# Moving the row-maximum subtraction to GpSimd and the exponential behind the transpose, with scratch rows stored in residue order

## The chip, the cores and the metric

The kernel runs on one core of one Trainium2 chip. A core has a matrix engine (TensorE, in the profile PE, with its weight loads as PEld), VectorE (DVE), ScalarE (ACT), GpSimd (POOL) and SyncE (SP), which here only issues DMAs. The metric is the device time of one execution in microseconds. The kernel before takes 710.51 us as the median of 3 runs (709.28 to 711.08).

## The reference

Two layers follow each other. The first is attention over 8 batches of 8 heads, 576 positions and 64 features per head. Four heads see a window of 32 positions back; the other four see every fourth position, 32 of them back. The second is a mixture of 8 experts: each of the 4608 tokens goes to one expert, in the order of its gate values, with at most 576 tokens for an expert.

```
mask_plain = (rel >= 0) & (rel < window)
mask_dil = (rel >= 0) & (rel < window * dilation) & (rel % dilation == 0)
scores = np.where(masks[None, :, :, :], scores, -1000000000.0)
scores = scores - np.max(scores, axis=-1, keepdims=True)
attn = np.exp(scores)
attn = attn / (np.sum(attn, axis=-1, keepdims=True) + 1e-09)
...
x = attn_out.transpose(0, 2, 1, 3).reshape(B * S, H * D)
...
h = np.maximum(x[mask] @ w1[e], 0.0)
out[mask] = h @ w2[e]
```

## The kernel before, in words

**Attention.** The work is cut into 32 units: 8 batches, two kinds of heads (kind 0 the plain window, kind 1 the dilated one), and two pairs of heads for each kind. Two heads lie on the two halves of the 128 partitions. A unit's 576 query rows are 9 chunks of 64 rows, and each chunk sees 96 keys. For kind 1 the host has sorted the positions by their remainder modulo 4 (the residue), so that a dilated window becomes a plain one; its rows therefore come out in residue order, while those of kind 0 are in token order.

The steps of a unit, with the names of their buffers and their lines: PE multiplies queries and keys into `pm` (`scores`, L380, chunks 0 to 4 and then 5 to 8); DVE adds the mask, scales, negates and takes the row's extreme in one instruction for each chunk (`most`, L386), which leaves the scores in `sc` and the extremes in `mx`; ACT takes the exponential of each chunk in place, with the extreme as its bias (`exps`, L392, nine instructions of 128x96); PE transposes `sc` three chunks at a time into `pS` (`turn`, L396); ACT copies that to `et` (L250, three of 96x384); PE multiplies `et` with the values, in whose tile a column of ones gives the row sums (`values`, L402, into `px`); DVE divides (`weigh`, L408 and L409) into `xs`. The pools have 3 tiles of `sc` and 3 of `et`.

When both units of a kind are done, SP stores `xs` to the scratch tensor `xd` in DRAM (`stores`), from which the second layer gathers rows later. PE also transposes `xs` (L463), ACT copies that to `xt` (on DVE, L477, at the very end), and PE multiplies `xt` with the gate weights (L497, L516, L552). The rows of kind 0 go to `xd` with two DMAs (L432). The rows of kind 1 have to be put back from residue order to token order, which takes 20 DMAs for a batch (L441): ten pieces, in which the chunk, the residue and the place in it stay the same, for each of the two halves of the partitions. The copy to `xt` puts them back in the same way, in two instructions each time.

**Routing and experts.** After the last gate value, DVE and PE search for the first expert's threshold (`alone`), lay out the list of its tokens (`digits`, `by_chunk` L952 on POOL, `by_row` L956 on ACT, `within` L960 on DVE, `place` L967 on PE, `indices` L976 to L979), and POOL gathers the token rows from `xd` with five indirect DMAs (L1131). The expert's weights come in 256 KB pieces into the tiles `raw` (SP, L1032), which lie in memory that attention used. ACT and DVE split them into a high and a low part (`w1h`, `w1l`, `w2h`, `w2l`, L1014 and L1015; some low parts by DMAs from POOL, L1042), PE multiplies (L1182, L1224), and POOL scatters the rows to the output with the same indices (L1250). Eight rounds of this follow each other.

**What sets the order.** Every step is an `Op` with an engine, a cost that is written in the code, and what it depends on. The planner (`Schedule.run`) plays the steps through with these costs and due times, and writes each engine's instructions down in the order that comes out. On the chip an engine takes its instructions in just that order and waits at each until its inputs are there. SP's queue is such an order too: a store that waits holds back the loads behind it. The loads of a batch go to one of two sets of `q`, `k` and `v` tiles, and wait until the batch before the last is done with it.

Of the kernel before, what the change touches and what calls it, by code (L numbers as in the profile page):

```python
# [25 lines left out]
NB = S // 64  # L26
SR = S // DIL
NCH = N // 128
NEG = -1e30
LG = 12  # L30
NK = 16
# [11 lines left out]
B_C = (0, 2500, 20000, 20000, 20000, 20000, 20000, 20000)  # L43
P_U, B_A, B_T, B_K, B_V, B_P, TOL_A, TOL_B, TOL_C, TOL_D = 4500, 8000, 4000, -5200, 4000, -105500, 650, 650, 300, 800
GR, N_S, N_E = ((0, 5), (5, 9)), 3, 3
MSZ = (128, 128, 128, 128, 64)
# [8 lines left out]


def consts():

# [3 lines left out]
    for kind in range(2):  # L62
        m = np.zeros((2, QB, NB, KB), np.float32)
        for c, (q0, k0) in enumerate(starts()):
            q, k = q0 + np.arange(QB)[:, None], k0 + np.arange(KB)[None, :]
# [160 lines left out]
def attention(tc, ctx, C, load_const, T, xd, Lt, R):  # L226
# [84 lines left out]
    class Unit:  # L311
# [16 lines left out]
        def build(self):  # L328
# [60 lines left out]

        def exps(self, c0, c1, mx, sc):  # L390
            for c in range(c0, c1):
                nc.scalar.activation(sc[:, c], sc[:, c], AF.Exp, bias=mx[:, c:c + 1], scale=-1.0)  # L392

# [17 lines left out]

    def pieces():

        out, at = [], 0
        while at < S:
            c, q = divmod(at, QB)
            r, i = divmod(at, SR)
            n = min(QB - q, SR - i)
            while q == 0 and n % QB == 0 and n + QB <= SR - i:
                n += QB  # L420
            out.append((c, q, r, i, n))
            at += n
        return out

    def stores(b, kind, xs):
        xb = xd[b * S:(b + 1) * S]
        out = []
        for half in range(2):
            f0 = 256 * kind + 128 * half
            src = xs[half * 64:half * 64 + 64].rearrange("p c a d -> p c (a d)")  # L430
            if kind == 0:
                out.append((lambda f0=f0, src=src: nc.sync.dma_start(  # L432
                    xb[:, f0:f0 + 128].rearrange("(c i) x -> i c x", i=QB), src), 64 * NB * 512))
                continue
            for c, q, r, i, n in pieces():
                k = -(-n // QB)
                w = min(n, QB)

                def put(c=c, q=q, r=r, i=i, k=k, w=w, src=src, f0=f0):
                    rows = xb[:, f0:f0 + 128].rearrange("(i r) x -> r i x", r=DIL)[r, i:i + k * w]  # L440
                    nc.sync.dma_start(rows.rearrange("(c i) x -> i c x", c=k), src[q:q + w, c:c + k])  # L441

                out.append((put, n * 512))
        return out
# [3 lines left out]
    def banks(un, xs, done, usex):  # L448
# [8 lines left out]
        for i in range(3):  # L457
            pt = Buf(PV)

            def turn(i=i, pt=pt):  # L460
                t = pt.tile[:, :384].rearrange("p (a c i) -> p a c i", a=2, c=3)
                for c in range(3):
                    nc.tensor.transpose(t[:, :, c], xs[:, 3 * i + c].rearrange("p a d -> p (a d)"), C["identf"])  # L463

            eng = "DVE" if b == B - 1 and kind and i else "ACT"

            def keep(i=i, pt=pt, f=nc.vector.tensor_copy if eng == "DVE" else act):
                t = pt.tile[:, :384].rearrange("p (a n) -> p a n", a=2)
                if kind == 0:
                    f(xt[:, :, 192 * i:192 * i + 192], t)  # L470
                    return
                x = xt.rearrange("p a (i r) -> p a r i", r=DIL)
                at = 0
                while at < 192:
                    r, j = divmod(192 * i + at, SR)
                    n = min(192 - at, SR - j)
                    f(x[:, :, r, j:j + n], t[:, :, at:at + n])  # L477
                    at += n
# [4 lines left out]
            k = un.op(eng, (450 if kind == 0 else 520) + 100 * (eng == "DVE"), keep, [t, *oldt], late)  # L483
            pt.users.append(k)
            xt_[b].append(k)
# [128 lines left out]
class Router:  # L614
# [355 lines left out]
    def indices(self, ps):  # L970
# [10 lines left out]
        return idx  # L981


def moe(tc, ctx, C, R, xd, w1, w2, out):
# [119 lines left out]
    def listing(r, sl):  # L1104
# [60 lines left out]
    def expert(r, X, box, W1, W2):  # L1165
# [48 lines left out]
        for m, n in sorted(enumerate(MSZ), key=lambda x: x[1] if r == NE - 1 else 0):  # L1214
# [33 lines left out]
            def put(m=m, n=n, y=y):  # L1248
                nc.gpsimd.memset(spacer, 0.0)
                s = nc.gpsimd.indirect_dma_start(  # L1250
                    out=out, out_offset=bass.IndirectOffsetOnAxis(ap=box[0][:n, m:m + 1], axis=0),
                    in_=y[:n], in_offset=None)
# [3 lines left out]

            usey.append(op("POOL", 1200, put, [c], B_S, lat=2300))

# [3 lines left out]

    X, BOX, W, EN = {}, {}, {}, {}

    def round_(r):
# [3 lines left out]
        en = st["fetch"] = EN[r] = op("SP", 100, lambda: fetch(r, R.eidx), [e])  # L1269
        ix, BOX[r] = settle(r, e)  # L1270
        X[r] = gather(r, ix, BOX[r])
        W[r] = [weights("1", r, f, [en]) for f in range(NF)]
# [15 lines left out]
def layout(inputs):  # L1288
# [7 lines left out]
    d = {  # L1296
        "in_qp": plain(q), "in_kp": plain(k),
        "in_qd": plain(apart(q)), "in_kd": plain(apart(k)),
# [58 lines left out]
```

## Time and profile before

| What | Value |
|---|---|
| median of 3 runs | 710.51 us |
| profiled execution, its time and its span | 706.26 us, 704.5 us |
| busy: PE, DVE, ACT, POOL | 652.6, 458.7, 341.1, 113.2 us |
| mean granted TensorE clock | 0.966 |
| exponentials L392 | 288 instructions, 81.5 us busy, 367 ns each |
| copies to `et` L250 | 96 instructions, 43.3 us busy, 485 ns each |
| mask and extreme L386 | 288 instructions, 253 ns each |
| stores of attention rows, L432 and L441 | 16 and 160 DMAs |

The span falls into three stages: attention up to about 197 us, where the last gate values are multiplied; routing for the first expert up to 230 us, where the first gather is issued; and the experts to the end. The profiled execution ran 4.25 us (0.6%) below the median of the others. PE's busy time is counted to the modelled end of each pipelined matmul, so that 98% busy still holds small gaps.

### The profile page before, as it was taken

The numbers are of one execution on the slowest core, as the hardware profiler recorded it, in microseconds if no ns is written. First come the engines' busy times: TensorE is split into PE (matmuls) and PEld (weight loads), VectorE is DVE, ScalarE is ACT, GpSimd is POOL, SyncE is SP. The second block draws the span as 40 slices with busy tenths as digits, with TensorE's granted clock in tenths as the row PEclk, the third lists the DMA queues.
The fourth block names the chain that finished last, engine by engine and source line by source line (L and its number), as shares of the span: only waits on it lengthen the run. The fifth ranks groups of instructions, "written<-read, shape, count | busy, mean of one in ns | idle before, by whom it ended". The sixth has DMA issues, their size and how long they took to land.

```text
span 704.5 us, 17467 instructions
## 1 busy us (share of the span) xinstructions
PE 652.6 (93%) x6553; PEld 556.9 (79%) x6553; DVE 458.7 (65%) x1939; ACT 341.1 (48%) x891; POOL 113.2 (16%) x162
## 2 busy tenths in 40 slices
PE   8789999998952899999999999999999999999995
PEld 5678788877741698798789789879978978988983
DVE  3537566665566699688589779868978955723300
ACT  5767897867601474376235333523524525424210
POOL 0000000000000332542311310310311131211011
PEclk9979999999965899999999999999999999999998
DMA  8996886795532684897213513511621484112001
GB/s 238 268 259 173 257 220 198 202 268 158 138 88 78 202 180 105 250 221 234 98 54 122 186 60 113 188 45 51 226 85 54 150 277 150 51 55 97 1 24 45
DMA packets 69882, 103.35 MB, mean 147 GB/s; under 512 B 8355, under 2 KB 41123, under 8 KB 69795
## 3 DMA queue, kind: packets, MB, share of 16 engines
q1 hardware_dynamic: 60454, 77.07, 37.1%
q0 software_dynamic: 9344, 25.17, 12.9%
q8 instruction: 51, 0.84, 0.5%
q14 instruction: 33, 0.27, 0.1%
HBM read 77.05 MB, written 18.87 MB: 136 GB/s over the span
## 4 chain that ended last, share of the span: by engine, by line
PE 57%; issue 12%; DMA 10%; ACT 6%; DVE 6%; SPq 3%; POOL 3%; POOLq 0%; DVEq 0%; ACTq 0%
PE ph L1182 21%; PE py L1224 14%; PE pm L380 5%; DMA raw<-in_moe_w 4%; PE px L402 4%; PE pS L396 3%; ACT sc L392 2%; SPq L441 2%; PE pz L655 2%; POOL xg L1131 2%; PE ptx L1145 2%; PE py L1227 1%; PE py L1229 1%; DMA k<-in_kp 1%; DMA v<-in_vd 1%
## 5 line engine op out<-in xcount | busy, mean ns | idle before, releaser
L1224 PE MATMUL py<-w2h,hb 128*128 128x512 f32 x512 | 171.4, 399 | 0.0
L1182 PE MATMUL ph<-xh,w1h 128*128 128x256 f32 (+1 forms) x512 | 138.7, 301 | 0.0
L1182 PE MATMUL ph<-xl,w1h 128*128 128x256 f32 (+1 forms) x512 | 136.2, 297 | 0.0
L1182 PE MATMUL ph<-xh,w1l 128*128 128x256 f32 (+1 forms) x512 | 136.1, 296 | 0.0
L1224 PEld LDWEIGHTS py<-w2h,hb 128*128 128x128 f32 x512 | 96.2, 188 | 19.7 <-ACT w2h L1014 0.7
L1014 ACT ACTIVATE hb<-ph 128x256 fp32r<-128x256 f32 (+2 forms) x192 | 59.6, 345 | 96.0 <-PE ph L1182 95.2
L1224 PE MATMUL py<-w2l,hb 128*128 128x512 f32 x256 | 100.4, 392 | 0.6 <-DVE w2l L1015 0.5
L1182 PEld LDWEIGHTS ph<-xh,w1h 128*128 128x128 f32 x512 | 91.5, 190 | 0.4
L1182 PEld LDWEIGHTS ph<-xh,w1l 128*128 128x128 f32 x512 | 91.6, 190 | 0.0
L1182 PEld LDWEIGHTS ph<-xl,w1h 128*128 128x128 f32 x512 | 91.5, 190 | 0.0
L392 ACT ACTIVATE sc<-sc,mx 128x96 f32<-128x96 f32 x288 | 81.5, 367 | 19.6 <-DVE mx L386 19.5
L386 DVE CUSTOM_DVE_ANT_0 sc<-pm,const 128x96 f32<-128x96 f32 x288 | 55.4, 253 | 43.8 <-PE pm L380 41.7
L1202 DVE SCALAR_TENSOR_TENSOR hb<-ph,hb 128x320 fp32r<-128x320 f32 (+1 forms) x128 | 57.6, 454 | 30.3 <-ACT hb L1014 28.9
L1014 ACT ACTIVATE y<-py 128x512 f32<-128x512 f32 (+1 forms) x40 | 23.8, 596 | 104.7 <-PE py L1224 90.7
L1250 POOL DMA_INDIRECT out<-y,idx x40 | 39.8, 996 | 203.9 <-ACT y L1014 143.2
L380 PE MATMUL pm<-k,q 64*64 64x96 f32 x1152 | 60.6, 252 | 4.0 <-DMA k<-in_kd 2.3
L380 PEld LDWEIGHTS pm<-k,q 64*64 64x64 f32 x1152 | 50.6, 136 | 11.7 <-issue 4.5
L1014 ACT ACTIVATE w1h<-raw 128x512 fp32r<-128x512 f32 x64 | 38.7, 628 | 39.2 <-DMA raw<-in_moe_w 39.0
L1224 PEld LDWEIGHTS py<-w2l,hb 128*128 128x128 f32 x256 | 48.2, 188 | 10.2 <-DVE w2l L1015 1.9
L952 POOL TENSOR_TENSOR rx<-oa,const 128x360 bf16<-128x360 bf16 x8 | 7.2, 904 | 294.5 <-DVE oa L947 294.5
L250 ACT ACTIVATE et<-pS 96x384 f32<-96x384 f32 x96 | 43.3, 485 | 22.2 <-PE pS L396 22.2
L396 PE MATMUL pS<-const,sc 128*96 128x128 f32 x288 | 45.1, 284 | 6.7 <-ACT et L250 6.5
(155 smaller groups left out, 977.2 us busy)
## 6 DMA issues: line engine op xcount, KB each, us to landing
raw<-in_moe_w SPq DMA_DIRECT2D x128, 256.0 KB, 4.7
v<-in_vp SPq DMA_DIRECT2D x8, 780.0 KB, 5.9
v<-in_vd SPq DMA_DIRECT2D x8, 780.0 KB, 10.0
xd<-xs SPq DMA_DIRECT2D x16, 288.0 KB, 8.4
w2l<-raw POOLq DMA_DIRECT2D x16, 256.0 KB, 4.4
q<-in_qp SPq DMA_DIRECT2D x7, 576.0 KB, 9.7
k<-in_kp SPq DMA_DIRECT2D x7, 576.0 KB, 8.7
q<-in_qd SPq DMA_DIRECT2D x7, 576.0 KB, 6.6
```

Of the source, the lines that this page charges most:

```text
L250: act = lambda o, i: nc.scalar.activation(o, i, AF.Copy)
L380: nc.tensor.matmul(pm[p, (c - c0) * KB:(c - c0 + 1) * KB], self.Q[c][p], self.K[c][p], start=True, stop=True)
L386: nc.vector.tensor_tensor_reduce(out=sc[:, c], in0=pm[:, (c - c0) * KB:(c - c0 + 1) * KB], in1=mm[:, c if self.kind else min(1, c)], scale ...
L392: nc.scalar.activation(sc[:, c], sc[:, c], AF.Exp, bias=mx[:, c:c + 1], scale=-1.0)
L396: nc.tensor.transpose(pt[:KB, 128 * c:128 * c + 128], sc[:, 3 * j + c], C["identf"])
L402: nc.tensor.matmul(px[64 * a:64 * a + 64, c - c0], self.E0[:, 128 * c + 64 * a:128 * c + 64 * a + 64], self.V[c][a], start=True, stop=True)
L441: nc.sync.dma_start(rows.rearrange("(c i) x -> i c x", c=k), src[q:q + w, c:c + k])
L1014: act = lambda o, i, f=AF.Copy: nc.scalar.activation(o, i, f)
L1182: nc.tensor.matmul(o, a[:, d * 128:d * 128 + 128], b[:, d, c0:c1], start=((d, i) == pairs[0]), stop=((d, i) == pairs[-1]))
L1202: hl = op("DVE", 335 if j == 0 else 400, lambda: nc.vector.scalar_tensor_tensor(hb[:, CAP + c0:CAP + c1], o, 0.0, hb[:, c0:c1], op0=OP.max ...
L1224: nc.tensor.matmul(py, x, w, start=(f + i == 0), stop=(f == NF - 1 and i == 2))
L1250: s = nc.gpsimd.indirect_dma_start(out=out, out_offset=bass.IndirectOffsetOnAxis(ap=box[0][:n, m:m + 1], axis=0), in_=y[:n], in_offset=None)
```

## The change

- The exponentials leave ACT's queue ahead of the transpose. In their place POOL subtracts the extreme from the scores, in place, with one `tensor_tensor` for each group of chunks (`shift`: 128x480 and 128x384), two for a unit.
- The transposed scores are then read by ACT out of PSUM: the three copies of 96x384 become three exponentials of 96x384 (`exps`). There are still 96 of them, and the 288 exponentials of 128x96 are gone.
- The host permutes the 64 query rows of each chunk of kind 0 by residue (`quads`), and their mask with them. The scratch tensor holds each batch's rows in residue order. Kind 1 is then stored with two DMAs for a batch, and kind 0 with eight (one for each residue and half, 16 partitions by 9 chunks). That is 10 in place of 22.
- The copies to `xt` are one instruction each; it is those of kind 0 that reorder now.
- The gathers take their indices as they are. For the scatter, POOL works out the token numbers from the indices in twelve small instructions for a round (`tokens`, tiles of 128x5).
- Costs and one due time (`B_TOK`) in the planner follow.

```diff
-                e = self.op("ACT", 175 * n, lambda c0=c0, c1=c1: self.exps(c0, c1, mx, sc), [d], B_A)
+                e = self.op("POOL", 240 * n, lambda c0=c0, c1=c1: self.shift(c0, c1, mx, sc), [d], B_A)
...
-                k = self.op("ACT", 380, lambda j=j, pt=pt: act(self.E0[:KB, 384 * j:384 * j + 384], pt.tile[:KB, :384]),
+                k = self.op("ACT", 400, lambda j=j, pt=pt: self.exps(j, pt.tile),
...
-        def exps(self, c0, c1, mx, sc):
-            for c in range(c0, c1):
-                nc.scalar.activation(sc[:, c], sc[:, c], AF.Exp, bias=mx[:, c:c + 1], scale=-1.0)
+        def shift(self, c0, c1, mx, sc):
+            nc.gpsimd.tensor_tensor(sc[:, c0:c1], sc[:, c0:c1], mx[:, c0:c1, None].to_broadcast([128, c1 - c0, KB]),
+                                    op=OP.subtract)
+
+        def exps(self, j, pt):
+            nc.scalar.activation(self.E0[:KB, 384 * j:384 * j + 384], pt[:KB, :384], AF.Exp, scale=-1.0)
...
-            for c, q, r, i, n in pieces():
...
+            n = QB // DIL
+            for r in range(DIL):
+                out.append((lambda r=r, rows=rows, src=src: nc.sync.dma_start(
+                    rows[SR * r:SR * r + SR].rearrange("(c j) x -> j c x", j=n), src[n * r:n * r + n]), n * NB * 512))
...
+    def tokens(self, idx):
...
+        whole(g, idx, SR)
+        whole(h, g, DIL)
+        e.tensor_scalar(t, idx, float(DIL), None, op0=OP.mult)
+        e.tensor_scalar(g, g, float(1 - S), None, op0=OP.mult)
+        e.tensor_tensor(t, t, g, op=OP.add)
+        e.tensor_scalar(h, h, float(S - DIL), None, op0=OP.mult)
+        e.tensor_tensor(t, t, h, op=OP.add)
+        e.tensor_copy(tok, t)
...
+        st["tok"] = op("POOL", 1500, lambda: box.append(R.tokens(box[0])), [ix], B_TOK)
...
-                    out=out, out_offset=bass.IndirectOffsetOnAxis(ap=box[0][:n, m:m + 1], axis=0),
+                    out=out, out_offset=bass.IndirectOffsetOnAxis(ap=box[1][:n, m:m + 1], axis=0),
```

The planner puts the instructions in a new order. First place: ACT around the first units of batch 1, whose scores are `sc_105` and `sc_106` (`et` and `xt` as above, `px` and `pS` the PSUM banks). Before:

```order
L392 ACTIVATE sc_105<-sc_105,mx_109 128x96 x9
L250 ACTIVATE xt_120<-px_134 128x2x48
L250 ACTIVATE xt_120<-px_134 128x288
L392 ACTIVATE sc_106<-sc_106,mx_110 128x96 x9
L250 ACTIVATE et<-pS_131 96x384
L250 ACTIVATE et<-pS_132 96x384
```

and now:

```order
L257 ACTIVATE xt_120<-px_133 128x2x192
L257 ACTIVATE xt_120<-px_134 128x2x192
L257 ACTIVATE xt_120<-px_135 128x2x192
L402 ACTIVATE et<-pS_131 96x384
L402 ACTIVATE et<-pS_132 96x384
```

Before, the exponentials of two whole units stand ahead of the first copy to `et`; now only copies to `xt` do.

Second place: the end of SP's queue in attention, the stores of the last batch (`xs_115` kind 0, `xs_117` kind 1). Before, with the second half of the last twenty left out:

```order
L432 DMA xd<-xs_115 64x9x128 x2
L441 DMA xd<-xs_117 64x2x128
L441 DMA xd<-xs_117 16x128
L441 DMA xd<-xs_117 48x128
L441 DMA xd<-xs_117 64x128
L441 DMA xd<-xs_117 32x128 x2
L441 DMA xd<-xs_117 64x128
L441 DMA xd<-xs_117 48x128
L441 DMA xd<-xs_117 16x128
L441 DMA xd<-xs_117 64x2x128 x2
```

and now, up to the first weights of the experts:

```order
L435 DMA xd<-xs_114 16x9x128 x8
L430 DMA xd<-xs_116 64x9x128 x2
L435 DMA xd<-xs_115 16x9x128 x8
L430 DMA xd<-xs_117 64x9x128 x2
L1274 TENSOR_LOAD eidx
L1045 ISA
L1045 DMA raw_2887<-in_moe_w 128x512
```

Two DMAs stand behind the very last rows in place of twenty, and ten are issued for the last batch in place of 22.

Third place: POOL in the first round of the experts, the end of the twelve small instructions (`gt`, `gg`, `gh` are their tiles, `tok` the result), which stand behind the five gathers:

```order
L988 TENSOR_SCALAR gt<-idx 128x5
L989 TENSOR_SCALAR gg<-gg 128x5
L990 TENSOR_TENSOR gt<-gt,gg 128x5
L991 TENSOR_SCALAR gh<-gh 128x5
L992 TENSOR_TENSOR gt<-gt,gh 128x5
L993 CAST tok<-gt 128x5
L1055 DMA w2l_2923<-raw_2895 128x512
```

Before, the `w2l` DMA followed the gathers and one small memset directly. In the experts PE, DVE, ACT and SP have the same order before and now, but for the names.

More of the change, by code (lines that the diff above doesn't have):

```diff
@@ L29 @@
 NEG = -1e30
+WHOLE = 1.5 * 2 ** 23
 LG = 12
@@ L44 @@
 P_U, B_A, B_T, B_K, B_V, B_P, TOL_A, TOL_B, TOL_C, TOL_D = 4500, 8000, 4000, -5200, 4000, -105500, 650, 650, 300, 800
+B_TOK = -10000
 GR, N_S, N_E = ((0, 5), (5, 9)), 3, 3
@@ L54, with quads @@
 QB, KB = 64, 96
+def quads():
+    return np.arange(QB).reshape(QB // DIL, DIL).T.reshape(-1)
 def consts():
@@ L64, in consts @@
         for c, (q0, k0) in enumerate(starts()):
-            q, k = q0 + np.arange(QB)[:, None], k0 + np.arange(KB)[None, :]
+            q, k = q0 + (np.arange(QB) if kind else quads())[:, None], k0 + np.arange(KB)[None, :]
             seen = (q >= k) & (q - k < WIN)
@@ L410, in weigh @@
                                     op=OP.mult)
[L412 to L423, printed above, removed]
     def stores(b, kind, xs):
@@ L430, in stores @@
             src = xs[half * 64:half * 64 + 64].rearrange("p c a d -> p c (a d)")
-            if kind == 0:
-                out.append((lambda f0=f0, src=src: nc.sync.dma_start(
-                    xb[:, f0:f0 + 128].rearrange("(c i) x -> i c x", i=QB), src), 64 * NB * 512))
+            rows = xb[:, f0:f0 + 128]
+            if kind:
+                out.append((lambda rows=rows, src=src: nc.sync.dma_start(
+                    rows.rearrange("(c i) x -> i c x", i=QB), src), 64 * NB * 512))
                 continue
-            for c, q, r, i, n in pieces():
[L436 to L443, printed above, removed]
+            n = QB // DIL
+            for r in range(DIL):
+                out.append((lambda r=r, rows=rows, src=src: nc.sync.dma_start(
+                    rows[SR * r:SR * r + SR].rearrange("(c j) x -> j c x", j=n), src[n * r:n * r + n]), n * NB * 512))
         return out
@@ L460, in turn @@
             def turn(i=i, pt=pt):
-                t = pt.tile[:, :384].rearrange("p (a c i) -> p a c i", a=2, c=3)
+                t = pt.tile[:, :384]
+                if kind:
+                    t = t.rearrange("p (a c i) -> p a c i", a=2, c=3)
+                else:
+                    t = t.rearrange("p (a r c j) -> p a c r j", a=2, c=3, r=DIL)
                 for c in range(3):
@@ L468, in keep @@
                 t = pt.tile[:, :384].rearrange("p (a n) -> p a n", a=2)
-                if kind == 0:
+                if kind:
                     f(xt[:, :, 192 * i:192 * i + 192], t)
[L471 to L478, printed above, removed]
+                else:
+                    x = xt.rearrange("p a (r n) -> p a r n", r=DIL)
+                    f(x[:, :, :, 48 * i:48 * i + 48], t.rearrange("p a (r n) -> p a r n", r=DIL))
             need = [x for k, x in enumerate(done) if (k % 2 == 0 and 3 * i < GR[0][1]) or (k % 2 and 3 * i + 3 > GR[1][0])]
@@ L482, in banks @@
             usex.append(t)
-            k = un.op(eng, (450 if kind == 0 else 520) + 100 * (eng == "DVE"), keep, [t, *oldt], late)
+            k = un.op(eng, 450 + 100 * (eng == "DVE"), keep, [t, *oldt], late)
             pt.users.append(k)
@@ L981, in indices, with whole @@
         return idx
+    def tokens(self, idx):
+        pw, e = self.pw, self.tc.nc.gpsimd
+        tok = pw.tile([128, NM], I32, name="tok", bufs=4)
+        g, h, t = (pw.tile([128, NM], F32, name="g" + x) for x in "ght")
+        def whole(o, x, d):
+            e.tensor_scalar(o, x, 1.0 / d, (0.25 - 0.5 * d) / d, op0=OP.mult, op1=OP.add)
+            e.tensor_scalar(o, o, WHOLE, None, op0=OP.add)
+            e.tensor_scalar(o, o, -WHOLE, None, op0=OP.add)
+        whole(g, idx, SR)
[6 more added lines that the diff above has]
+        e.tensor_copy(tok, t)
+        return tok
 def moe(tc, ctx, C, R, xd, w1, w2, out):
@@ L1255, in put @@
                 scat.append(s)
-            usey.append(op("POOL", 1200, put, [c], B_S, lat=2300))
+            usey.append(op("POOL", 1200, put, [c, toks[r]], B_S, lat=2300))
     def fetch(r, eidx):
@@ L1261, in fetch @@
                               skip_runtime_bounds_check_because="the index is the place of a maximum among NE flags")
-    X, BOX, W, EN = {}, {}, {}, {}
+    X, BOX, W, EN, toks = {}, {}, {}, {}, {}
     def round_(r):
@@ L1270, in round_ @@
         ix, BOX[r] = settle(r, e)
+        toks[r] = st["tok"]
         X[r] = gather(r, ix, BOX[r])
@@ L1296, in layout @@
     d = {
-        "in_qp": plain(q), "in_kp": plain(k),
+        "in_qp": plain(q.reshape(B, H, NB, QB, D)[:, :, :, quads()].reshape(B, H, S, D)), "in_kp": plain(k),
         "in_qd": plain(apart(q)), "in_kd": plain(apart(k)),
```

## The prediction

> **What bounds the kernel now.** I read the stretches of the span first, since the change sits in one stage. In each row stand the stretch, its length, and the busy time of PE, PEld, DVE, ACT and POOL with their instruction counts, then the granted clock, the DMA share and GB/s.
>
> ```profile
> 10.00:30.00 20.00, 17.43 (x320) 14.77 (x316) 10.51 (x75) 14.31 (x44) 0.00 (x0) 1.00 1.07 271
> 60.00:150.00 90.00, 87.72 (x1532) 72.87 (x1530) 59.42 (x419) 73.18 (x234) 0.00 (x0) 1.00 0.75 217
> 150.00:197.00 47.00, 40.64 (x770) 32.15 (x770) 27.00 (x173) 30.81 (x95) 0.00 (x0) 1.00 0.65 178
> 210.00:230.00 20.00, 6.10 (x102) 4.34 (x102) 13.03 (x49) 2.27 (x4) 1.44 (x1) 0.50 0.30 84
> ```
>
> From 60 to 150 us PE is busy 97%, ACT 81%, POOL not at all. From 150 to 197 PE idles 6.4 us. From 210 to 230 it hardly works, and its clock is at half. Next the groups of instructions from 60 to 150 us: how much work that was, and whose.
>
> ```profile
> L392 ACT ACTIVATE sc<-sc,mx 128x96 f32<-128x96 f32 x146 | 41.3, 368 | 2.9 <-DVE mx L386 2.8
> L386 DVE CUSTOM_DVE_ANT_0 sc<-pm,const 128x96 f32<-128x96 f32 x144 | 27.7, 253 | 16.7 <-PE pm L380 16.5
> L250 ACT ACTIVATE et<-pS 96x384 f32<-96x384 f32 x51 | 22.9, 486 | 12.8 <-PE pS L396 12.7
> ```
>
> 144 instructions of L386, nine for a unit, are 16 units: the pace is 90/16 = 5.63 us a unit. ACT spends 73.18/16 = 4.57 on each, 41.3/16.2 = 2.55 of it on the exponentials. What PE alone would need I take from the chain of waits (start, length, what; it counts each fp32 matmul as two, with their weights), where PE runs without a gap; the last row is a group from 20 to 230 us, the gate transposes.
>
> ```profile
> 66.82 1.63 PE pm L380 x36
> 65.62 1.20 PE px L402 x36
> 108.72 0.79 PE pS L396 x6
> 74.17 0.46 PE pS L396 x3
> 82.36 1.13 PE px L463 x9
> 102.66 1.18 PE px L497 x16
> 98.45 2.38 ACT sc L392 x9
> L516 PE MATMUL px<-const,L 128*128 128x128 f32 x31 | 5.7, 285 | 0.0
> ```
>
> A unit is 1.63 + 1.20 + 0.79 + 0.46, half of a 1.13 and a quarter of a 1.18: 4.94 us. The gate transposes add 5.7 us over 30 units, 0.19; with the small counts behind them (L647) I estimate 0.35 us, so 5.3 us. PE is thus near its own limit in the steady part, and ACT's exponentials cost about 0.3 us a unit there. Elsewhere they cost more. The order of time at the start, PE's instructions with the idle time before them in brackets, and stretches around it:
>
> ```profile
> 32.53 0.86 PE L396 MATMUL pS<-const,sc 128*96 128x128 f32 x6
> 37.18 0.88 PE L396 MATMUL pS<-const,sc 128*96 128x128 f32 x3 [3.80 <-ACT et L250]
> 40.00:42.00 2.00, 2.00 (x30) 1.66 (x28) 0.98 (x10) 0.84 (x4) 0.00 (x0) 0.50 1.11 218
> 44.00:46.00 2.00, 2.00 (x22) 1.61 (x22) 0.70 (x8) 1.27 (x4) 0.00 (x0) 0.60 0.88 205
> ```
>
> PE stands still for 3.8 us while ACT takes 18 exponentials of two units ahead of the copy that PE needs, and then runs at half clock until about 45 us. The last view is the chain at the end of attention, with SP's queue and POOL from the order of time:
>
> ```profile
> 174.33 8.68 DMA v<-in_vd
> 188.31 3.10 DMA xd<-xs
> 193.16 0.50 DVE xs L409
> 208.28 12.79 SPq L441 DMA_DIRECT2D xd<-xs  x20
> 219.56 3.29 DVE L960 TENSOR_TENSOR ob<-si,const 128x768 bf16<-128x768 int32 x3
> 219.73 1.44 POOL L952 TENSOR_TENSOR rx<-oa,const 128x360 bf16<-128x360 bf16 x1 [218.60 <-DVE oa L947]
> 220.46 2.12 DMA xd<-xs
> 222.91 2.64 DMA raw<-in_moe_w
> 225.81 1.15 ACT w1h L1014 x2
> 226.96 0.50 ACT rx L956
> 227.59 0.78 PE ptx L967 x18
> 230.17 1.27 POOL xg L1131
> ```
>
> The attention rows are ready at about 193.7 us, but SP issues the last twenty stores from 208.28 to 221.1. The first weights follow them, ACT splits two pieces, and only then does it make `rx`, which PE needs for the list of tokens. The first gather waits for a train of stores that has nothing to do with it.
>
> **The change part by part.** *ACT, exponentials.* Removed: 288 instructions, 2.55 us a unit. The three copies of 96x384 become exponentials of the same shape. No row has that form: a copy takes 486 ns, the lower bound. For the upper one I need what an exponential with its bias column costs over a copy, from two copies of other widths:
>
> ```profile
> 239.63 0.38 ACT L1014 ACTIVATE hb<-ph 128x256 fp32r<-128x256 f32 x1 [0.40 <-PE ph L1182]
> 234.52 0.60 ACT L1014 ACTIVATE xh<-py 128x512 fp32r<-128x512 f32 x1 [6.34 <-PE py L1145]
> ```
>
> They put a copy of 96 columns at 0.24 us; the exponential of 96 takes 368 ns, 0.13 more, so 0.61 us. I take 0.55, nearer the copy in shape. At the dearer end ACT has 4.57 - 2.55 + 0.38 = 2.4 us a unit: 45% of the new pace, so it hides.
>
> *POOL, the subtraction.* POOL ran nothing in attention, so the price comes from its only `tensor_tensor`:
>
> ```profile
> L952 POOL TENSOR_TENSOR rx<-oa,const x8: 789/794/1435, 219.7 to 603.9; 128x360 bf16<-128x360 bf16 x8
> ```
>
> 794 ns for 360 columns is 2.2 ns a column, and 1435 ns (beside DVE's `ob`) is 4.0. Groups of 480 and 384 columns cost 1.06 + 0.85 = 1.9 us a unit at the median and 3.4 at the top. I take 2.1: the operands differ (f32 for bf16), the second operand is repeated in both. POOL is then 40% busy, and a unit waits 1.06 us before its first transpose where ACT took 5/9 of 2.38 = 1.3. Behind a shift on POOL only the next shift waits. In the hole at 33.4 us ACT no longer has anything ahead of `et`; PE has the next unit's scores (1.63 us) to cover 0.95 of DVE and 1.06 of POOL.
>
> *PE and DVE.* The instruction counts stay, but for two copies of `xt` fewer on DVE. PE's transposes of `xs` for kind 0 write PSUM in pieces of 16 columns: at least nothing, at most what half clock would cost (1.13 us more for each of 8 batches, 9 us). I take nothing, since the columns stay the same.
>
> *Stores.* 176 become 80. The row of SP's queue (min, median, max ns to issue), and two of the page's DMA list (KB, us to landing):
>
> ```profile
> L441 SPq DMA_DIRECT2D xd<-xs x160: 302/457/3304, 48.3 to 220.5; - x160
> xd<-xs SPq DMA_DIRECT2D x16, 288.0 KB, 8.4
> xd<-xs SPq DMA_DIRECT2D x32, 64.0 KB, 7.1
> ```
>
> Twenty at the median are 9.1 us of SP's queue for a batch, eight are 3.7. The loads queued behind come 5.5 us sooner, more where stores wait for a landing: the chain above goes through a load of 8.68 us, the stores behind it, and a last landing of 3.10 us that DVE waits for with the next `xs`. A store from 16 partitions of nine chunks is 72 KB; those of 64 KB land in 7.1 us, those of 288 KB in 8.4, so it frees `xs` no later than those do now.
>
> *The end of attention.* Ten stores at 0.5 to 0.65 us are issued within 6 us of the last rows and land some 8 us later, so the first weights are there by 193.7 + 6 + 8 + 3 = 211, and split by 212. `rx` needs `oa`, whose end starts POOL's half at 219.73. So ACT makes its half at once, POOL's half ends at 221.2, and `place` starts behind `ob` at 222.95 in place of 227.59: 4.6 us.
>
> *Token numbers.* Twelve small POOL instructions for a round: at least 0.09 us each (the memset of one element), at most 0.79 (L952). I take 0.15, 1.8 us. The memset, and what hides the twelve:
>
> ```profile
> 236.95 0.09 POOL L1023 MEMSET raw<- 1x1 f32 x1
> 245.67 0.99 POOL L1042 DMA_DIRECT2D w2l<-raw  x1 [8.63 <-ACT w2l L1040]
> 296.99 0.97 POOL L1250 DMA_INDIRECT out<-y,idx  x1 [5.04 <-ACT y L1014]
> ```
>
> In the first two rounds they fall into these idle times of 8.6 and 5.0 us, later into longer ones. Uncovered, they would put 1.8 us ahead of a `w2l` DMA or a scatter; at the upper price the second gap is overrun by 4.4 us, once.
>
> **The sum.** Against the profiled execution's 706.26 us. Steady part: I expect a pace of 5.4 rather than 5.3, since POOL's handover is new; 0.23 x 16 units = 3.6. The hole: 3.8 us, and 9.5 us at half clock that a full clock does in 4.7, together 8.5; DMA is at a share of 1.1 here, so loads may become the next thing to be late; I take 5.0. From 150 to 197: half of the 6.4 idle, 3.2, as a drain at the end remains. Routing: 4.6. Experts: 0. Together 16.4, so 689.9 us, and as the median of the runs shown is 4.25 us above that execution, 694.
>
> The Trainium skill (TensorE: Matmul & The Clock Gate, Part 1: The HAM clock gate) says that the clock halves after an idle window of about 3.4 us. The trace agrees with a gap of 3.8 us. By that rule a gap only half a microsecond shorter would give the whole clock loss back, and the term of the hole would be 8.5.
>
> **The rivals.** *Loads become the bound* (0.20). For: 10 to 30 us runs at a DMA share of 1.07, 271 GB/s. A batch moves 4.06 MB of loads and 1.18 MB of stores (sizes by the page's DMA list), 5.24 MB; at 271 GB/s that is 19.3 us against 4 x 5.3 = 21.2 on PE, and a load may start only when its tile is free. Against: 217 GB/s from 60 to 150. Then the first stretch gives 1, the steady part 1.5, the tail 2, routing 4.6: 9 us, 701.5.
>
> *Everything closes* (0.12). Pace 5.3 (0.33 x 16 = 5.3), the whole hole (8.5), the tail but for a drain of 2.4 (4.0), routing 4.6, the start 0.6: 23 us, 687.5. For: the gap of 3.8 us is just long enough for the clock. Against: loads at share 1.1 there.
>
> *POOL and DVE block each other: slower* (0.08). For: in the rows at 219.6, `rx` took 1435 ns and not 794 while DVE ran `ob`. If `most` does that to a shift in attention, each of a unit's two groups waits for about half a shift, 0.5 us, and half of that reaches PE in the fixed order: 0.5 us a unit, 16 us in all, less the 4.6 of routing: 11 us slower, 721.5. It decides once DVE's 59.42/16 = 3.7 us and POOL's 1.9, end to end 5.6, exceed the pace. Against: `most` reads `pm` from PSUM, and `ob` two inputs from SBUF. The Trainium skill (SBUF — State Buffer, Who interferes with whom) says that a VectorE instruction with two SBUF inputs blocks GpSimd's reads and one with a single SBUF input does not; by that rule this rival is nearly out, and no row here shows a shift beside `most`.
>
> *The forecast* has 0.60.
>
> **How the numbers follow.** About 0.3%, 2.1 us, is what a measurement of this kernel can tell from no change. Forecast and second rival are faster beyond that, and nearly all of the first: 0.60 + 0.12 + 0.18 = 0.90. Same: 0.04, slower 0.06, from the third rival and the weak end of the first. The range goes from the second rival, 2 us below it for the store rows, to 4 us above the first, for uncovered token numbers: 685 to 706. The slower rival is left out.
>
> **What would show it.** Right: ACT about 45% busy from 60 to 150 us; shifts at 1.0 to 1.2 and 0.8 to 1.0 us; no stretch at half clock between 20 and 150 us; the last store within 10 us of the last rows; PE's `ptx` right behind `ob`; attention's last gate values near 185 us. Wrong: shifts near 1.9 us with `most` stretched (third rival), waits of PE for `q`, `k` or `v` (first), or a gather that still waits for `raw`.

## The result and the profile after

The changed kernel takes 686.50 us (median of 4 runs, 684.72 to 686.70), the kernel before on the same chip 709.89 us (708.68 to 711.08): a ratio of 0.9665, with a 95% interval of 0.9640 to 0.9689. The profiled execution took 686.65 us with a span of 684.9, against 706.26 and 704.5 before. Medians and ratios leave out single executions in a slower state, such as those of 901.94, 1044.80 and 822.26 us in three of the runs below.

| up to or between | before | after |
|---|---|---|
| last gate values in `Lt` | 197.82 us | 184.73 us |
| from there to the first gather | 32.35 us | 27.36 us |
| from there to the end of the span | 474.3 us | 472.8 us |

The stretches of the changed kernel, in the columns of the prediction's first view:

```profile
30.00:60.00 30.00, 26.90 (x475) 21.97 (x474) 15.57 (x125) 9.73 (x22) 10.82 (x12) 1.00 0.96 246
60.00:150.00 90.00, 89.40 (x1579) 74.03 (x1574) 63.97 (x459) 31.46 (x72) 31.77 (x36) 1.00 0.98 275
150.00:197.00 47.00, 40.49 (x844) 32.55 (x841) 30.52 (x173) 13.61 (x31) 7.82 (x9) 0.91 0.37 86
```

No clock is lost from 30 to 150 us, ACT's share fell to 35%, POOL's rose to 35%, and the DMA share in the steady part went from 0.75 to 0.98: loads now run ahead, and the last of them is issued at 149.8 us where it was 174.3. The groups of instructions from 60 to 150 us, with shapes kept apart:

```profile
L393 DVE CUSTOM_DVE_ANT_0 sc<-pm,const 128x96 f32<-128x96 f32 x162 | 31.2, 253 | 12.4 <-PE pm L387 12.1
L402 ACT ACTIVATE et<-pS 96x384 f32<-96x384 f32 x48 | 22.0, 485 | 47.0 <-PE pS L406 46.2 <-PE pz L639 0.6
L398 POOL TENSOR_TENSOR sc<-sc,mx 128x480 f32<-128x480 f32 x18 | 17.9, 995 | 39.5 <-DVE mx L393 35.4 <-DVE rec L418 3.0 <-DVE Lt L514 1.1
L398 POOL TENSOR_TENSOR sc<-sc,mx 128x384 f32<-128x384 f32 x18 | 14.9, 829 | 23.1 <-DVE mx L393 22.4 <-DVE rec L418 0.8
```

The exponential out of PSUM costs 485 ns, as much as the copy had; the two subtractions 1.82 us a unit; `most` is as short as before.

How far attention has come cannot be read from one line, since the scores of later units run ahead by a varying amount. I count units by three of PE's lines, scores (36 matmuls a unit), transposes (9) and values (36), and take the mean. From 60 to 150 us, before and then after:

```profile
L380 PE MATMUL pm<-k,q 64*64 64x96 f32 x576 | 29.6, 247 | 0.0
L396 PE MATMUL pS<-const,sc 128*96 128x128 f32 x151 | 23.1, 280 | 1.4 <-ACT et L250 1.4
L402 PE MATMUL px<-v,et 97*64 97x65 f32 x596 | 22.3, 226 | 0.6 <-ACT xt L250 0.2
```

```profile
L387 PE MATMUL pm<-k,q 64*64 64x96 f32 x624 | 31.5, 247 | 0.2 <-DVE mx L393 0.2
L406 PE MATMUL pS<-const,sc 128*96 128x128 f32 x146 | 22.8, 280 | 0.1
L412 PE MATMUL px<-v,et 97*64 97x65 f32 x612 | 22.9, 226 | 0.0
```

That is 16.45 units before (16.0, 16.8, 16.6) and 16.85 after (17.3, 16.2, 17.0): 5.47 and 5.34 us a unit. By 60 us the same count gives 8.93 and 9.94. (The 5.0 us a unit of some expectations below is an earlier count of mine from `most` alone: 162 instructions, 18 units.) The count is rough: from 60 to 150 us scores say 1.3 units more than before and transposes 0.6 fewer.

The view that the prediction lacked is SP's queue in order of time through a whole batch. Before, and then after:

```profile
125.31 16.62 SPq L441 DMA_DIRECT2D xd<-xs  x20
142.03 0.36 SPq L257 DMA_DIRECT2D v<-in_vp  x1
...
152.91 14.90 SPq L441 DMA_DIRECT2D xd<-xs  x20
...
192.09 14.70 SPq L441 DMA_DIRECT2D xd<-xs  x20
206.89 1.29 SPq L432 DMA_DIRECT2D xd<-xs  x2
```

```profile
119.57 10.19 SPq L435 DMA_DIRECT2D xd<-xs  x8
129.86 0.38 SPq L264 DMA_DIRECT2D v<-in_vd  x1
...
137.89 11.33 SPq L435 DMA_DIRECT2D xd<-xs  x8
...
172.25 3.87 SPq L435 DMA_DIRECT2D xd<-xs  x8
182.30 1.27 SPq L430 DMA_DIRECT2D xd<-xs  x2
```

Before, SP hardly pauses between 37 and 221 us: each row starts where the one ahead of it ends. From the train of stores at 75.52 us to the one at 174.94 lie four batches, 24.9 us each, while PE needs 4 x 5.34 = 21.4. SP falls behind, and the last rows, ready at 194.2, are stored from 206.89 on. After, trains start at 59.25, 80.43, 98.37, 119.57 and 137.89 us, 19.7 us a batch, and the last store is issued 0.03 us behind its rows.

A queue without gaps is no proof in itself, since a row of SP's also holds waits for transfers, and after the change it has few gaps too; the experiments had to show it. The trace can part issues from waits. SP's DMAs share eight semaphores (counters that tell when a transfer has landed) in turn, and of the 208 DMAs of the changed kernel for which the trace holds both times none starts before the one eight places ahead has landed. Of the 16.62 us of twenty stores at 125.31 us, 11.68 are issues and 4.17 waits for such a landing; of the 10.19 us of eight stores at 119.57 us after the change, 4.76 and 5.23. In the trains of before at 192.09 and 208.28 us, which no load crosses, nothing waits for one: twenty issues with the short steps between them take the 14.70 and 12.79 us.

The end of routing, in order of time, in the changed kernel:

```profile
203.52 1.48 SPq L1045 DMA_DIRECT2D raw<-in_moe_w  x3
206.38 3.29 DVE L952 TENSOR_TENSOR ob<-si,const 128x768 bf16<-128x768 int32 x3
206.77 1.15 ACT L1027 ACTIVATE w1h<-raw 128x512 fp32r<-128x512 f32 x2 [24.04 <-DMA raw<-in_moe_w]
207.83 0.58 ACT L948 ACTIVATE rx<-oa,const 128x360 bf16<-128x360 bf16 x1
208.55 0.69 PE L959 MATMUL ptx<-rx,ob 128*128 128x40 bf16 x12 [4.39 <-ACT rx L948]
209.73 0.38 PE L959 MATMUL ptx<-rx,ob 128*128 128x40 bf16 x6 [0.49 <-DVE ob L952]
212.09 1.29 POOL L1145 DMA_INDIRECT xg<-xd,idx  x1 [4.10 <-DVE cap L884]
```

`ptx` ends right behind `ob`. ACT's `rx` still stands behind two pieces of weights (`w1h`), but these have landed by 206.77 us, when `ob` has just begun; before, they came 6 us behind the start of `ob` (225.81 and 219.56).

### The profile page after: what moved, and what is told of

It is laid out like the page before. It is cut to its first block, busy times and chain, and to the rows that moved or that the text cites. A ratio compares the mean times of both kernels' runs of the same rounds, so it can differ in the third digit from the quotient of the medians.

```text
span 684.9 us, 17314 instructions
## 1 busy us (share of the span) xinstructions
PE 645.1 (94%) x6551; PEld 553.7 (81%) x6553; DVE 459.1 (67%) x1937; ACT 260.8 (38%) x581; POOL 201.7 (29%) x322
## 4 chain that ended last, share of the span: by engine, by line
PE 65%; issue 12%; DMA 8%; DVE 6%; POOL 4%; ACT 2%; SPq 1%; POOLq 0%; DVEq 0%; ACTq 0%
PE ph L1196 20%; PE py L1238 16%; PE pm L387 7%; PE px L412 6%; PE pS L406 5%; DMA raw<-in_moe_w 5%; PE px L460 3%; POOL xg L1145 2%; PE ptx L1159 2%; PE pz L647 2%; POOL out L1264 1%; DMA v<-in_vp 1%; PE px L489 1%; PE py L1241 1%; PE py L1243 1%
## 5 line engine op out<-in xcount | busy, mean ns | idle before, releaser
L398 POOL TENSOR_TENSOR sc<-sc,mx 128x480 f32<-128x480 f32 (+1 forms) x64 | 57.6, 910 | 116.3 <-DVE mx L393 110.2
L1264 POOL DMA_INDIRECT out<-y,tok x40 | 40.0, 1000 | 166.6 <-ACT y L1027 91.7
L402 ACT ACTIVATE et<-pS 96x384 f32<-96x384 f32 x96 | 43.9, 485 | 92.7 <-PE pS L406 91.8
L387 PE MATMUL pm<-k,q 64*64 64x96 f32 x1152 | 57.3, 247 | 1.6 <-DVE rec L418 0.7
L387 PEld LDWEIGHTS pm<-k,q 64*64 64x64 f32 x1152 | 49.0, 133 | 9.7 <-issue 5.4
L1145 POOL DMA_INDIRECT xg<-xd,idx x40 | 40.5, 1013 | 53.2 <-PE ph L1196 31.2
L1028 DVE TENSOR_TENSOR w2l<-raw,w2h 128x512 fp32r<-128x512 f32 x48 | 31.6, 686 | 21.6 <-ACT w2h L1027 21.2
```

The lines of the kernel that those rows point to most:

```text
L387: nc.tensor.matmul(pm[p, (c - c0) * KB:(c - c0 + 1) * KB], self.Q[c][p], self.K[c][p], start=True, stop=True)
L398: nc.gpsimd.tensor_tensor(sc[:, c0:c1], sc[:, c0:c1], mx[:, c0:c1, None].to_broadcast([128, c1 - c0, KB]), op=OP.subtract)
L402: nc.scalar.activation(self.E0[:KB, 384 * j:384 * j + 384], pt[:KB, :384], AF.Exp, scale=-1.0)
L1145: nc.gpsimd.indirect_dma_start(out=xg[:n], out_offset=None, in_=xd, in_offset=bass.IndirectOffsetOnAxis(ap=box[0][:n, m:m + 1], axis=0))
L1264: s = nc.gpsimd.indirect_dma_start(out=out, out_offset=bass.IndirectOffsetOnAxis(ap=box[1][:n, m:m + 1], axis=0), in_=y[:n], in_offset=None)
```

## The experiments

Each ratio is to the kernel before as measured beside that run (medians 710.51, 709.83 and 709.40 us). "Units" is the count above, by 60 us and from 60 to 150; "gate" the end of the last gate values.

| run | median us | ratio (95%) | units by 60 | 60 to 150 | gate us |
|---|---|---|---|---|---|
| before | 709.89 | 1 | 8.93 | 16.45 | 197.8 |
| exponentials alone | 709.78 | 0.9997 (0.9962 to 1.0031) | 9.85 | 15.11 | 207.2 |
| stores alone | 696.36 | 0.9807 (0.9751 to 0.9864) | 9.30 | 16.11 | 191.1 |
| both: after | 686.50 | 0.9665 (0.9640 to 0.9689) | 9.94 | 16.85 | 184.7 |
| after, twenty stores | 709.49 | 0.9994 (0.9960 to 1.0028) | 10.00 | 14.20 | 206.8 |
| before, values once | 692.97 | 0.9779 (0.9700 to 0.9858) | 9.70 | 16.86 | 189.1 |
| exponentials, values once | 686.31 | 0.9678 (0.9583 to 0.9773) | 10.52 | 16.74 | 182.1 |
| after, values once | 681.22 | 0.9600 (0.9532 to 0.9668) | 10.52 | 17.11 | 179.2 |

**The exponentials alone.** The kernel before, with the first half of the change:

```diff
-                e = self.op("ACT", 175 * n, lambda c0=c0, c1=c1: self.exps(c0, c1, mx, sc), [d], B_A)
+                e = self.op("POOL", 240 * n, lambda c0=c0, c1=c1: self.shift(c0, c1, mx, sc), [d], B_A)
-                k = self.op("ACT", 380, lambda j=j, pt=pt: act(self.E0[:KB, 384 * j:384 * j + 384], pt.tile[:KB, :384]),
+                k = self.op("ACT", 400, lambda j=j, pt=pt: self.exps(j, pt.tile),
```

> The kernel before with one half of the change: GpSimd subtracts the maximum and ScalarE takes the exponential behind the transpose; the stores stay as they were, twenty for a batch of kind 0, and no token numbers are made. My theory (ScalarE's relief makes most of what attention won, about 8 to 12 of its 13.1 us; the stores make routing's 5 us and a little of attention): 8 to 12 us below the kernel before, about 700 us, the distance from the last gate values to the first gather near the 32.4 us of the kernel before, SP's queue busy with the last twenty stores as long as before. Rival (PE was full and the loads wait behind the stores, so that the stores make nearly all): at most 2 us below the kernel before, about 708 us, and a DMA share from 60 to 150 us near the 0.75 of before.

No gain at all; my theory's 8 to 12 us are not there. The gap at 33 us does close (9.85 units by 60 us, as with the whole change), but from 60 to 150 us the kernel does 1.3 units less than before. Around one stop, in order of time, and the clock there:

```profile
96.48 2.56 SPq L435 DMA_DIRECT2D xd<-xs  x2
...
100.67 0.49 DVE L412 TENSOR_TENSOR xs<-px,rec 128x320 f32<-128x320 f32 x1 [4.50 <-DMA xd<-xs]
...
101.21 1.03 PE L405 MATMUL px<-v,et 97*64 97x65 f32 x14 [4.16 <-DVE xs L412]
```

```profile
100.00:104.00 4.00, 2.79 (x27) 1.59 (x27) 2.21 (x7) 0.49 (x1) 0.00 (x0) 0.50 0.97 279
```

DVE cannot write the next `xs` before the old one's stores have landed, PE waits 4.16 us for DVE, and the clock halves. Two more such gaps follow, of 4.90 us up to 152.84 (for `xs`) and 3.67 up to 182.44 (for the loads of `v`). The stall that ACT had caused came back from SP. The distance from the last gate values to the first gather was 29.1 us, and not near the 32.4 that I expected.

**The stores alone.** The changed kernel, with the exponentials back on ACT ahead of the transpose and the copy behind it:

```diff
-                e = self.op("POOL", 240 * n, lambda c0=c0, c1=c1: self.shift(c0, c1, mx, sc), [d], B_A)
+                e = self.op("ACT", 175 * n, lambda c0=c0, c1=c1: self.exps(c0, c1, mx, sc), [d], B_A)
```

> The other half: the stores in residue order, ten a batch, with the token numbers, and the exponentials on ScalarE ahead of the transpose as before, no work of attention on GpSimd. My theory: 5 to 9 us below the kernel before, about 703 us, of which 5 from the end of attention to the first gather (near 27.4 us, as with the whole change); the gap of PE at 33 us and its half clock stay. Rival (the stores make nearly all): 18 to 21 us below, about 690 us. If both halves are additive, this run and the one with the exponentials alone sum to the 23.4 us of the whole change; if the loads and ScalarE take turns as the bound, the two sum to clearly less.

14.2 us less, between both theories. In the trace 6.7 lie up to the gate values and 4.8 from there to the first gather (191.14 and 218.65 against 197.82 and 230.17); the rest is the profiled execution of before, which lay below its median. The two halves give 0 and 14, together 23: clearly more than their sum, the case that the expectation names for loads and ScalarE taking turns as the bound. ACT's stall stays, as expected:

```profile
PE pS L403 <- ACT et L257: 8.4, 10, 3.3
```

**Twenty stores again.** The changed kernel with each store of kind 0 cut by chunks, the same rows to the same places, twenty a batch:

```diff
+                cs = (0, 5, 9) if r % 2 else (0, 3, 6, 9)
+                for a, z in zip(cs, cs[1:]):
+                    out.append((lambda r=r, a=a, z=z, rows=rows, src=src: nc.sync.dma_start(
+                        rows[SR * r:SR * r + SR].rearrange("(c j) x -> j c x", j=n)[:, a:z],
+                        src[n * r:n * r + n, a:z]), n * (z - a) * 512))
```

> The changed kernel with each of the eight stores of kind 0 cut by chunks into two or three, so that a batch has twenty again, as before, with the same rows at the same places. Theory (the number of issues: in the kernel before SP's queue works without a gap from 37 to 221 us, a train of twenty takes it 12.8 to 16.6 us, and loads stand behind it): almost all that the stores gave is lost, 703 to 713 us, as with the exponentials alone; the last twenty stores again take about 12.8 us of SP's queue and are issued well after the last rows. Rival (the size and order of the pieces and how they land, not their number): at most 692 us.

709.49 us: the whole gain of the change is gone, 23 us for twelve more DMAs a batch. SP's queue and the waits up to 205 us:

```profile
172.09 16.14 SPq L437 DMA_DIRECT2D xd<-xs  x20
190.61 12.67 SPq L437 DMA_DIRECT2D xd<-xs  x20
...
206.03 11.55 SPq L437 DMA_DIRECT2D xd<-xs  x20
```

```profile
DVE xs L419 <- DMA xd<-xs: 11.8, 4, 4.0
PE px L412 <- DVE xs L419: 9.4, 5, 2.8
```

A batch takes SP 26.0 us again (trains from 68.04 to 172.09, four batches), and the rows ready at 203.4 are stored up to 218.9. It is the number of stores, not the order of rows. The train at 190.61, with no load issued behind it, still takes 12.67 us where eight stores took 3.87: 10.87 of it are issues, and 1.03 waits of three stores for the landing of the DMA eight places ahead.

**Values loaded once.** In the kernel before, in the one with the exponentials alone, and in the changed kernel, every batch uses the values of batch 0:

```diff
-            V = VT[self.kind][:, s]
+            V = VT[self.kind][:, 0]
-                load_values(b, kind)
+                ready["V", kind, b] = ready["V", kind, 0]
```

> The kernel before, with the values of batch 0 used for every batch (14 value loads of 780 KB left out, the output is another). Theory (before, ScalarE and the loads take turns as the bound, so that neither alone gives much): 2 to 6 us below the kernel before. Rival (the loads behind the stores were the whole of it): 12 us below or more, as much as the new stores gave (14.2). Second rival (ScalarE alone bounds it): 0 to 1 us.

> The kernel before with the exponentials behind the transpose and the old stores, as in the run with the exponentials alone, and with the values of batch 0 used for every batch: 14 of 16 value loads (780 KB each, 10.9 MB) are left out, so the output is another. The run with the exponentials alone gained nothing. Theory (it runs out of loads: the twenty stores of a batch hold SP's queue and the freed ScalarE makes PE ask for data sooner): 8 to 15 us below the run with the exponentials alone, 697 to 703 us, with PE's gaps before v and xs gone. Rival (the way over GpSimd costs PE as much as ScalarE gives back, in this order of work): within 3 us of that run, about 710 us, and no more gain than the kernel before has from the same omission.

> The changed kernel, with the values of batch 0 used for every batch (14 value loads of 780 KB left out, the output is another). Theory (from 60 us on PE is the bound at 5.0 us a unit, DMA share 0.98 notwithstanding; loads are late only between 10 and 60 us): 1 to 4 us below the changed kernel, none of it from 60 to 150 us, where the pace stays 5.0. Rival (loads are the new bound of the steady part): 8 us or more below, pace under 4.8.

The kernel before gains 16.9 us, the one with the exponentials alone 23.5, where I had expected 8 to 15. The rival expectation holds for before: the loads in SP's queue, much more than ACT, held it back. It was not the DMA engines' capacity, of which before used 0.75 from 60 to 150 us. The same stretch with values once, of the kernel before and then of the changed one:

```profile
60.00:150.00 90.00, 87.38 (x1549) 72.45 (x1548) 59.58 (x416) 72.74 (x234) 0.00 (x0) 1.00 0.50 150
```

```profile
60.00:150.00 90.00, 89.99 (x1628) 75.09 (x1625) 63.42 (x426) 32.75 (x76) 29.43 (x33) 1.00 0.55 151
```

With SP relieved either way, moving the exponentials is worth 6.7 us (692.97 to 686.31) or 9.9 (696.36 to 686.50); with SP full, nothing. The changed kernel still gains 5.3 us from fewer loads, more than expected, half a unit of it by 60 us, where loads remain late. From 60 to 150 us PE is busy for 89.99 of 90 us: there it is the bound.

**The subtraction: twice, not at all, and on VectorE.** In the changed kernel the `tensor_tensor` of `shift` is written twice, or left out, or given to DVE:

```diff
-            nc.gpsimd.tensor_tensor(sc[:, c0:c1], sc[:, c0:c1], mx[:, c0:c1, None].to_broadcast([128, c1 - c0, KB]),
+            nc.vector.tensor_tensor(sc[:, c0:c1], sc[:, c0:c1], mx[:, c0:c1, None].to_broadcast([128, c1 - c0, KB]),
                                     op=OP.subtract)
```

> The whole change, but each subtraction on GpSimd is done twice in a row (the scores are then shifted by twice the maximum, so the output isn't the reference's). It adds about 1.7 us of GpSimd work to each unit, 55 us over 32 units, and 0.82 to 0.91 us of delay between each maximum and its transpose. My theory: GpSimd goes from 35% to 70% from 60 to 150 us and the order by hand has room for the delay: 0 to 3 us above the changed kernel. Rival (my slower case, in its size: the handover through GpSimd reaches PE in the fixed order): half of the 0.9 us a unit and more, 12 to 28 us above.

> The whole change without the subtraction: the row maximum is left out, the transpose takes the scores as they are (the output isn't the reference's). GpSimd does nothing in attention, and SP's wait of 2.7 us for a memset behind the subtractions is gone too. My theory (the subtraction is hidden): 0 to 2 us below the changed kernel, most of it near 30 us. Rival (the handover costs PE something in each unit): 5 us or more below, with a pace under the 5.0 us a unit of the changed kernel from 60 to 150 us.

> The changed kernel with the subtraction on VectorE (planned at 115 ns a chunk) in place of GpSimd. Theory (VectorE is busy 71% from 60 to 150 us and the subtraction adds about 1 us a unit, 19%, so it is near 90% there and its small operations come late): 3 to 12 us above the changed kernel. Rival (a shorter way, without two handovers, for PE's transposes): 0 to 3 us below it.

(A factor that all of a row has in common leaves again with the division by the row's sum; the first two expectations are wrong where they say that the output is another.) Without the subtraction: 686.37 us, ratio 0.9635 (0.9566 to 0.9704), no gain. Twice: 700.79 us, 0.9872 (0.9806 to 0.9937), 14.3 us above the changed kernel; my theory's 0 to 3 fell, and the slower rival's size of 12 to 28 is right for two. The groups on POOL and PE's wait for them:

```profile
L400 POOL TENSOR_TENSOR sc<-sc,mx 128x480 f32<-128x480 f32 (+1 forms) x32 | 29.2, 914 | 2.5
L398 POOL TENSOR_TENSOR sc<-sc,mx 128x384 f32<-128x384 f32 (+1 forms) x31 | 28.1, 906 | 31.6 <-DVE mx L393 31.6
```

```profile
PE pS L408 <- POOL sc L400: 10.1, 14, 1.8
```

So in this order of instructions one subtraction of 0.9 us a group is covered and a second is not: the slack behind the first lies below 0.9 us, though POOL is busy for only 55.94 of the 90 us. On VectorE it takes 602 ns a group and the kernel 687.63 us, 0.9671 (0.9617 to 0.9726), which can't be told from 686.50; neither expectation, 3 to 12 us above or 0 to 3 below, shows:

```profile
L398 DVE TENSOR_TENSOR sc<-sc,mx 128x480 f32<-128x480 f32 (+1 forms) x34 | 19.3, 602 | 0.1
```

```profile
60.00:150.00 90.00, 89.35 (x1598) 75.51 (x1596) 77.72 (x473) 31.95 (x76) 0.00 (x0) 1.00 0.96 262
```

VectorE is at 86% there, as the expectation had it, and PE at 99%. Relief for ACT was needed, GpSimd was not.

**The stores on ScalarE's queue.** The changed kernel with `nc.scalar.dma_start` for the ten stores:

```diff
-                    usex.append(op("SP", 300, f, Unit.xsd, -u * P_U - 5000, dma=n / D_R))
+                    usex.append(op("ACT", 460, f, Unit.xsd, -u * P_U - 5000, dma=n / D_R))
```

> The changed kernel with the stores of the attention rows issued from ScalarE's queue (planned at 460 ns each), so that no load stands behind a store that waits for rows or for its turn. Theory (SP's queue still holds loads back in the changed kernel, where leaving out the value loads won 5.3 us): 681 to 685.5 us. Rival (DMA engines are full anyway, and the 4.6 us of issues a batch come ahead of exponentials that PE waits for): 688 to 700 us.

715.88 us, 1.0072 (1.0038 to 1.0106), slower than both kernels and beyond both expectations. ACT now stands behind the trains, and PE behind ACT:

```profile
ACT et L402 <- DMA xd<-xs: 22.4, 3, 11.1
...
PE px L460 <- ACT xt L257: 10.2, 3, 6.7
PE px L412 <- ACT xt L257: 10.1, 1, 10.1
```

It is one more sign that a train of stores blocks the queue in which it stands. The Trainium skill (DMA: Bandwidth & Descriptors, Issuing engines are not separate DMA queues) says that issuing from several engines only saves the sequencer's time, which is usually small beside the DMA. In the kernel before that time was a bound of attention, and here what it costs ACT's queue is more than it gives SP's.

**Token numbers, and a memset.** Two more edits of the changed kernel: the scatter takes the places in the list (no `tokens`), and `nc.gpsimd.memset(wgp, 0.0)` stands ahead of all units.

> The changed kernel without the token numbers: the scatter uses the places in the list, so that each batch's rows leave in residue order (another output). Twelve small GpSimd instructions a round, 3.4 us, eight rounds, are gone. Theory (hidden in GpSimd's idle time): within 1 us of the changed kernel. Rival (they come late for a second-layer weight or a scatter): 2 to 5 us below it.

> The changed kernel with one move: the memset of the gate weights' tile stands first on GpSimd, and not behind the subtractions of the first units, where SP's queue waits 2.7 us for it at 29 to 32 us. Theory (the loads between 10 and 60 us are late, so what SP loses there PE loses): 1 to 2.5 us below the changed kernel, 684 to 685.5. Rival (what SP loses is caught up, since DMA engines have a share of 0.96 to 1.06 there and are behind anyway): within 0.5 us.

688.97 us, 0.9707 (0.9622 to 0.9791), and 688.52 us, 0.9722 (0.9643 to 0.9802): neither can be told from the changed kernel, and neither is a gain. The token numbers are hidden. For the memset my premise was a misreading. The profile put SP's 2.7 us down to POOL, but the memset had been done long before SP's row began:

```profile
12.78 0.20 POOL L589 MEMSET wgp<- 128x128 f32 x1
```

What held the row stays open. The DMA eight places ahead, whose semaphore it waits for too, had landed at 28.61 us, before the row began at 28.99; and in the kernel before, where this memset ran at 0.93 us and POOL did nothing after it, the row took 2.29 us as well.

## Why the prediction was right, and where it was wrong

The time lies 7.5 us below the forecast of 694 and inside the range, next to the rival "everything closes" (687.5). By its steps:

| term | forecast | measured | how |
|---|---|---|---|
| the hole and the half clock | 5.0 | 5.4 | 1.01 units more by 60 us, at 5.34 |
| steady part | 3.6 | 2.1 | (5.47 - 5.34) x 16.45 |
| tail of attention | 3.2 | 5.6 | the rest of 13.1 us |
| routing | 4.6 | 5.0 | 32.35 - 27.36 |
| experts | 0 | 1.5 | 474.3 - 472.8; other runs lie between 471.7 and 477.5, so no effect of the change |
| sum | 16.4 | 19.6 | |
| median above the profiled execution | 4.25 | -0.15 | 686.50 - 686.65 |

The first three rows share the 13.1 us that the last gate values come sooner (197.82 to 184.73). How they share them rests on the rough count of units; only their sum is read directly.

- **More than half of the miss is the last row**: I carried the offset of the kernel before over, whose profiled run lay 4.25 us below its median.
- **The step that failed is "What bounds the kernel now".** I read PE at 97% and ACT at 81% and laid hole and pace to the exponentials, with the stores as a help at the end. SP's queue was never totalled, though the quoted train of 12.79 us for twenty stores belonged to it. The runs show two limits, one behind the other: SP with its twenty stores, and behind it ACT's exponentials. Taking away the second alone gave 0 us, the first alone 14.2, both 23.4. That the sum came out well is luck: 8.6 of its 16.4 us, hole and pace, were laid to an edit that gains nothing without the stores.
- **The price of the stores** was the median of an issue, 457 ns, times twenty: 9.1 us. A train took 12.79 to 16.62 us, and cost is what the train occupies. Uncrossed by loads, twenty take 12.67 and eight 3.87 us: 8.8 us less, where I had 5.5. Between loads, where both wait for landings, a batch's cycle on SP shrank by 5.2 us (24.9 to 19.7). The larger tail is theirs, as far as the count goes: with the stores alone it stands at 25.41 units by 150 us, as before (25.38), and the last gate values come 6.7 us sooner.
- **The pace before** of 5.63 us was read from one line, `most`, whose 16 units are the lowest of the counts. PE's own need of 5.3 us was right: after, 5.34 with PE busy for 89.40 of 90 us.
- **The exponential** cost 0.485 us and not 0.55; ACT is at 35%, not 45%. It changed nothing.
- **The subtraction** is 1.82 us a unit, below the 2.1 taken, and hidden. That a handover may cost PE was right in its mechanism; the point from which it decides lies between one subtraction and two.
- **POOL and DVE blocking each other** did not come: `most` takes 253 ns with the subtractions, without them, and before, and no subtraction took more than 1.10 us, where `rx` beside `ob` had gone from 0.79 to 1.44. The rule of the Trainium skill that the prediction cites there (SBUF — State Buffer, Who interferes with whom) agrees with these runs.
- **PE's transposes in pieces of 16 columns** cost nothing, as the prediction took it: the transposes of `xs` (L460) last 270 to 330 ns, and before 272 to 332.
- **The clock.** PE's longest gaps between 30 and 150 us are now 0.99 and 1.66 us, and the clock stays at 1.00. With the stores alone the gap was 3.34 us, and the clock stood at 0.50 from 37.6 to 41.0 us, where before, behind the gap of 3.80, it had stood there from 35.4 to 45.6. So half a microsecond off the gap gave back two thirds of the stretch; the prediction, by the Trainium skill (TensorE: Matmul & The Clock Gate, Part 1: The HAM clock gate), had all of it. The skill's figure of about 3.4 us is not a sharp edge here: with the subtraction twice, a gap of 1.81 us up to 40.43 was followed by 0.50 until 43.9.
- **Loads become the bound** was half right: they are what is left (5.3 us), and with the old stores the queue that holds them cancelled all of ACT's relief. (The bytes of a batch are 5.34 MB, not 5.24: the loads are 4 x 576 + 2 x 877.5 = 4059 KB of 1024 bytes. At 271 GB/s that is 19.7 us, not 19.3, which changes nothing.)
- **Routing** came out, by a detail that was wrong: the first weights wait for the expert's index and not only for the stores: where SP is free they are issued 18.8 to 18.9 us behind the last gate values (184.73 to 203.52 after, 206.82 to 225.70 with twenty stores). With twenty stores and the new order the distance from gate values to gather is 27.5 us too (206.82 to 234.28), since SP is done there, at 218.9, before that index is known.
- **Token numbers** take 3.4 us a round, not 1.8, in idle time.

What stays open: why some issues of an uncrossed train take 1.1 to 1.7 us (three of twenty at 190.61 us, four at 192.09 before) where the median is 423 ns. Nothing was run to show it.

## What to carry to other kernels

Total a DMA queue like an engine: from one batch's first store to the next one's, against what the busiest engine needs for that batch; here twelve more DMAs of the same bytes cost as much as the whole change had won. When one limit stands behind another, removing the rear one alone shows nothing, so an edit that "gains nothing" alone may be the half that another one needs. Price a train of instructions by the time that the train occupies, not by its median times its count, and check a wait's named releaser against its own end before building on it.

## What the runs showed of the hardware that I had not expected

- 480 to 384 columns of f32 with a repeated second operand cost GpSimd 995 and 829 ns, VectorE 602 on the mean of the two: GpSimd is only 1.5 times as slow.
- ACT's exponential of 96x384 out of PSUM costs no more than its copy did, 485 ns each; ahead of the transpose, with a bias column, the same scores had cost nine times 368 ns.
- Twelve more DMAs a batch, with the same bytes, cost 23 us over eight batches: 2.9 us a batch; the loads, and at the end the first weights, stand behind them in the same queue.
- What a gap of PE costs is not told by its length. The stretches at half clock around the gaps of 3.34, 4.16 and 3.80 us lasted 3.4 us (stores alone), 6.8 (exponentials alone, 99.5 to 106.3) and 10.2 (before).
